# Pooled queries transposed by DMA, eight lanes for the MoE tail, and shorter score bursts chosen by backlog, in a fused attention and MoE kernel

## The chip, the cores and the metric

One core of a Trainium2 chip runs the whole program. The metric is the device time of one execution in microseconds (us). The span in a profile is 1.7 to 1.8 us shorter than that time. Runs of one kernel differ by 1 to 2% (39 runs of the kernel before in one job: 403.58 to 410.49 us), and with one core a run counts as slow when it is over 1.5% above the fastest of its kernel; only fast runs are compared. Ratios are the mean time of one kernel's fast runs over the mean of the other kernel's fast runs of the same rounds, so they are not quite the ratios of the medians quoted beside them.

## The reference

```python
# q, k, v: (8, 8, 1152, 64);  x: 4608 tokens x 512;  w1, w2: 512 x 1024;  w_out: 1024 x 512
q_pool = q.reshape(B, H, S // 2, 2, D).mean(axis=3)               # 576 queries a head
scores = scale * np.matmul(q_pool, k.transpose(0, 1, 3, 2))
attn = softmax(scores)                                            # (max, exp, sum)
x = np.matmul(attn, v).transpose(0, 2, 1, 3).reshape(B * 576, 512)
g = np.maximum(x @ w1, x @ w2)
out = g @ w_out
```

## The kernel before

Thirty-two pairs of heads, four pairs to a batch, run through TensorE (PE), the exponential on ScalarE (ACT), and PE again. Pooled queries, keys and values are prepared by GpSimd (POOL). As soon as a batch is through attention, its 576 tokens become MoE work, in blocks of 512 tokens. The kernel writes `max(x w1, x w2) w_out` as `relu(x (w1 - w2)) w_out + x (w2 w_out)`, so the MoE has a first layer ("h" jobs) and an output ("p" jobs).

The kernel uses eight PSUM banks of 512 FP32 columns. Six are three score buffers of two banks; two are "lanes" for everything else. The order in which PE does things is fixed when the program is built, by a greedy scheduler with its own rough clock:

```python
sps = [psum([P, 2, 512], f"sps{g}") for g in range(3)]     # score buffers
fb = [psum([P, 512], f"fb{g}") for g in range(2)]          # lanes

def qtrans(i):                 # pooled queries of pair i, transposed by PE through a lane
    def go(e, m):
        for u in range(QU):    # 9
            last = e.transpose(mb[:, u * HP:(u + 1) * HP], qp[s][:, u, :, :]..., ident[0:HP, 0:HP])
    def evac(m):
        dve(lambda e: e.tensor_copy(qpT[s][:, :], mb[:, 0:SQ]), ...)

def scores(g):                 # one group: 512 score columns for each of two heads, 64 rows each
    for i, t, lo, hi, col in pieces(g):
        for h in range(2):
            e.matmul(sps[r][:, h, col:col + hi - lo], kT[i % 3][rows(h), t, :], qpT[i % 2][rows(h), lo:hi], ...)

while p_end[0] < NTOK:
    # ... fill both lanes from the queues
    ready, stall = burst_now(BURST)               # BURST = 3 groups
    if ready and stall <= 0.1:                    # all their score buffers (nearly) free
        emit_burst(ready)
    elif fresh:                                   # else a piece of lane work that can start now
        emit_unit(...)
    else:
        # ... a smaller burst, if it saves more than 0.25 us of waiting
```

The softmax here doesn't subtract the row's maximum and nothing guards it: scores larger than these inputs give would overflow.

## Time and profile before

| | before |
|---|---|
| time, median of 3 runs | 407.5 us (406.59 to 410.68) |
| span of the profiled run, mean granted clock | 405.7 us, 0.992 |
| PE, ACT, DVE busy | 93%, 78%, 38% of the span |
| last scores end, last matmul ends | 346.8 us, 401.6 us |
| bursts of scores, by the built order | 118 |

The page gives averages over three stages with different limits: the start (to about 60 us, waiting for loads), the stretch in which attention and MoE share PE (to 346.8 us), and the tail of MoE alone. The lines on which this rests stand in the prediction below.

### The profile page before, as it was taken

How to read it: one execution, taken by the hardware profiler on the slowest of the kernel's cores; microseconds unless marked ns; L12 is line 12 of the kernel's file. 1: busy time of each engine (PE TensorE's matmuls, PEld its weight loads, DVE VectorE, ACT ScalarE, POOL GpSimd, SP SyncE). 2: the span in 40 equal slices, each digit the busy share in tenths (PEclk: the TensorE clock that was granted, in tenths of full speed). 3: DMA queues.
4: the chain of work that ended last, by engine and by line, in shares of the span. 5: the costliest groups of instructions: out<-in, count | busy, mean ns of one | idle time of the engine just before them, and what ended most of it. 6: DMA issues, size and time to landing. Idle time of an engine off the chain costs nothing.

```text
span 405.7 us, 11812 instructions
## 1 busy us (share of the span) xinstructions
PE 379.2 (93%) x5253; PEld 220.9 (54%) x5253; DVE 154.7 (38%) x310; ACT 317.3 (78%) x355; POOL 162.7 (40%) x135
## 2 busy tenths in 40 slices
PE   2886899999999998999999999999999999999895
PEld 1464465646554655565555555556555565544552
DVE  2458635342344333423243324422542244253221
ACT  3975889999998798989999999999999999400220
POOL 1458975526543563426545436435645110000000
PEclk9996999999999999999999999999999999999999
DMA  7999999647399979975799869998993520221322
GB/s 271 411 401 395 396 305 276 209 151 228 84 221 278 374 174 215 326 169 161 141 331 272 228 143 279 300 309 197 246 306 60 107 61 2 52 56 29 75 53 52
DMA packets 77091, 84.63 MB, mean 209 GB/s; under 512 B 49648, under 2 KB 50160, under 8 KB 77040
## 3 DMA queue, kind: packets, MB, share of 16 engines
q1 hardware_dynamic: 77040, 83.87, 74.6%
q8 instruction: 41, 0.67, 0.7%
q14 instruction: 10, 0.08, 0.1%
HBM read 62.91 MB, written 9.44 MB: 178 GB/s over the span
## 4 chain that ended last, share of the span: by engine, by line
PE 83%; DVE 7%; ACT 5%; DMA 3%; issue 1%; SPq 1%
PE fb L598 23%; PE fb L366 21%; PE sps L417 18%; PE fb L571 16%; ACT et L424 5%; PE fb L318 2%; PE fb L536 2%; DMA xT<-xnat 1%; DVE stage L582 1%; DVE wd L508 1%; DMA qraw<-in_q_dram 1%; DVE xnat L378 1%; DVE wo L512 1%; DVE stage L612 1%; PE fb L337 1%
## 5 line engine op out<-in xcount | busy, mean ns | idle before, releaser
L424 ACT ACTIVATE et<-sps 128x1024 bf16<-128x1024 f32 (+1 forms) x336 | 308.2, 998 | 32.4 <-PE sps L417 31.7
L292 POOL TENSOR_TENSOR qp<-qraw 64x576 bf16<-64x576 f32 x62 | 88.7, 1431 | 79.9 <-PE fb L318 65.6
L417 PE MATMUL sps<-qpT,kT 64*128 64x64 bf16 (+7 forms) x1152 | 98.5, 294 | 7.0 <-ACT et L424 4.3
L366 PEld LDWEIGHTS fb<-vE,et 128*128 128x128 bf16 x2880 | 93.6, 98 | 14.6 <-issue 7.3
L366 PE MATMUL fb<-vE,et 128*128 128x65 bf16 x2880 | 100.0, 194 | 0.1
L571 PE MATMUL fb<-xT,wd 128*128 128x512 bf16 (+3 forms) x352 | 73.9, 342 | 3.4 <-DMA xT<-xnat 0.9
L598 PE MATMUL fb<-wo,stage 128*128 128x512 bf16 x288 | 75.5, 380 | 0.0
L417 PEld LDWEIGHTS sps<-qpT,kT 64*128 64x128 bf16 x1152 | 43.8, 96 | 53.6 <-issue 22.5
L299 POOL TENSOR_SCALAR vE<-vraw 128x1152 bf16<-128x1152 f32 x32 | 38.1, 1191 | 76.2 <-issue 62.2
L582 DVE TENSOR_SCALAR stage<-fb 128x512 bf16<-128x512 f32 (+3 forms) x76 | 47.6, 628 | 40.9 <-PE fb L571 39.8
L376 DVE RECIPROCAL rc<-fb 128x5 f32<-128x5 f32 x64 | 12.5, 195 | 109.3 <-PE fb L366 109.3
L571 PEld LDWEIGHTS fb<-xT,wd 128*128 128x128 bf16 x352 | 28.5, 97 | 38.2 <-DVE stage L582 10.2
L612 DVE COPY stage<-fb 128x512 f32<-128x512 f32 x32 | 22.1, 690 | 57.9 <-PE fb L598 57.5
L598 PEld LDWEIGHTS fb<-wo,stage 128*128 128x128 bf16 x288 | 25.4, 98 | 28.2 <-issue 3.9
L268 POOL TENSOR_SCALAR kbf<-kraw 128x1152 bf16<-128x1152 f32 x31 | 36.2, 1167 | 7.5 <-DMA kraw<-in_k_dram 7.5
L598 PE MATMUL fb<-w,xT 128*128 128x512 bf16 x144 | 37.6, 380 | 0.8 <-DVE xnat L378 0.4
L378 DVE TENSOR_TENSOR xnat<-fb,rc 128x320 bf16<-128x320 f32 x64 | 31.5, 492 | 2.2
L609 ACT COPY stage<-fb 128x512 f32<-128x512 f32 x4 | 2.3, 586 | 31.6 <-PE fb L598 31.6
L325 DVE COPY qpT<-fb 128x576 bf16<-128x576 bf16 x32 | 14.5, 454 | 20.6 <-PE fb L318 20.6
L598 PEld LDWEIGHTS fb<-w,xT 128*128 128x128 bf16 x144 | 12.8, 97 | 17.1 <-DVE xnat L378 1.6
L318 PEld LDWEIGHTS fb<-ident,qp 64*128 64x128 bf16 x288 | 11.2, 97 | 12.7 <-DVE stage L582 4.2
L318 PE MATMUL fb<-ident,qp 64*128 64x64 bf16 x288 | 14.2, 194 | 3.1 <-DVE kT L344 3.1
(27 smaller groups left out, 68.9 us busy)
## 6 DMA issues: line engine op xcount, KB each, us to landing
qraw<-in_q_dram SPq DMA_DIRECT2D x32, 576.0 KB, 5.7
vraw<-in_v_dram SPq DMA_DIRECT2D x32, 576.0 KB, 7.1
kraw<-in_k_dram SPq DMA_DIRECT2D x31, 576.0 KB, 8.3
out_dram<-stage SPq DMA_DIRECT2D x72, 128.0 KB, 2.4
xT<-in_moe_w_dram SPq DMA_DIRECT2D x4, 512.0 KB, 9.5
stage<-in_moe_w_dram SPq DMA_DIRECT2D x4, 512.0 KB, 14.7
stage<-in_moe_w_out_dram SPq DMA_DIRECT2D x4, 512.0 KB, 14.5
xT<-xnat SPq DMA_TRANSPOSE x30, 2.5
```

The lines of the kernel that those rows point to most:

```text
L268: op("POOL", lambda g: g.tensor_scalar(kbf[s][:, :, :, :].rearrange("p t h d -> p h t d"), kraw[r][:, :, :, :], 1.0, 1.0, ALU.mult, ALU.mu ...
L292: op("DVE" if i == 0 else "POOL", lambda g, half=half, a=a: g.tensor_tensor(qp[s][:, :, half, :], a[:, :, 0, :], a[:, :, 1, :], ALU.add), ...
L299: op("POOL", lambda g: g.tensor_scalar(vE[r][:, :, :, 0:D].rearrange("p t h d -> p h t d"), vraw[r][:, :, :, :], 1.0, 1.0, ALU.mult, ALU.m ...
L318: last = e.transpose(mb[:, u * HP:(u + 1) * HP], qp[s][:, u, :, :].rearrange("p h d -> p (h d)"), ident[0:HP, 0:HP])
L366: last = e.matmul(fb[m][:, sb * 66:sb * 66 + 65], et[:, a:a + P], vE[vs][:, t, half, 0:65], start=(t == 0), stop=(t == NT - 1))
L378: dve(lambda e: e.tensor_tensor(xnat[xs][:, :, c:c + D], a[:, :, 0:D], rc[half][:, :].unsqueeze(2).to_broadcast([P, NCH + 1, D]), ALU.mult ...
L417: last = e.matmul(sps[r][:, h, col:col + hi - lo], kT[i % 3][rows(h), t, :], qpT[i % 2][rows(h), lo:hi], start=True, stop=True)
L424: op("ACT", lambda e: e.activation(et2[:, :, c:c + z - a], sps[r][:, :, a - g * W:z - g * W], EXP, scale=scale), r=[f"s{r}"], w=keys + [f" ...
L571: return e.matmul(fb[m][:, 0:size], wd[:, ct, ft * P:(ft + 1) * P], xT[:, ct, n0:n1], start=(ct == 0), stop=(ct == NC_ - 1))
L582: dve(lambda e: e.tensor_scalar_max(gT[:, ft, g0:g0 + size], fb[m][:, 0:size], 0.0), [f"f{m}"], w, 0.1 + size / 960.0)
L598: return e.matmul(fb[m][:, :], lhs, rhs, start=(j == 0), stop=(j == NC_ + NF - 1))
L612: dve(lambda e: e.tensor_copy(osb[o][:, :], fb[m][:, :]), [f"f{m}"], [f"osb{o}", f"f{m}"], 0.63)
```

## The change

The intent has three parts. From the sixth pair on, a DMA transposes the pooled queries, so PE and DVE need not. Once the last scores are done, the six score banks become lanes as well. And a burst holds three groups only while more than 800 tokens of MoE work are waiting, otherwise two. With the third goes a smaller margin: a smaller burst than this is put in when it saves 0.15 us of waiting instead of 0.25. The runs below change rule and margin together, except e10 to e12, which keep the margin. The rest of the diff is bookkeeping (a third buffer for the transposed queries, jobs that may now finish out of order).

```diff
-        qpT = [sbuf([P, SQ], BF16, f"qpT{s}") for s in range(2)]
+        qpT = [sbuf([P, SQ], BF16, f"qpT{s}") for s in range(3)]
+        fb += [sps[g][:, half, :] for g in range(3) for half in range(2)]
+        def qtrans_dma(i):
+            s, z = i % 2, i % 3
+            op("SP", lambda e: e.dma_start_transpose(
+                qpT[z][:, :].rearrange("p (u x) -> p u x", x=HP),
+                qp[s][:, :, :, :].rearrange("p u h d -> p (u h d)")),
+                r=[f"qp{s}.0", f"qp{s}.1"], w=[f"qpT{z}"], dma=f"d_qT{z}", cost=0.8, mode="t")
...
-        BURST = 3
+        LAG = 800
+        Q_PE = 5
...
+                if i + 2 >= Q_PE:
+                    later(f"qp{i % 2}.1", lambda: (qtrans_dma(i + 2), q_done.add(i + 2)), margin=1.5)
...
+        def more_banks():
+            for g in range(3):
+                for half in range(2):
+                    m = 2 + 2 * g + half
+                    lane[m] = None
+                    plan.writer[f"f{m}"] = plan.writer[f"s{g}"]
+                    plan.readers[f"f{m}"] = set(plan.readers[f"s{g}"])
...
+        def burst_size():
+            done = [b for b in range(B) if all(av_half.get(b * NHP + j) == 2 for j in range(NHP))]
+            return 3 if len(done) * SQ - p_end[0] > LAG else 2
...
+            if nxt == NGR:
+                more_banks()
...
-            for kk in (0, 1):
+            for kk in lane:
-            ready, stall = burst_now(BURST)
+            ready, stall = burst_now(burst_size())
...
-                if ready and stall < wait - 0.25:
+                if ready and stall < wait - 0.15:
```

More of the change, by code (lines that the diff above doesn't have):

```diff
@@ L324, in evac @@
                 mb = fb[m][:, :].bitcast(BF16)
-                dve(lambda e: e.tensor_copy(qpT[s][:, :], mb[:, 0:SQ]),
-                    [f"f{m}"], [f"qpT{s}", f"f{m}"], 0.4)
+                dve(lambda e: e.tensor_copy(qpT[i % 3][:, :], mb[:, 0:SQ]),
+                    [f"f{m}"], [f"qpT{i % 3}", f"f{m}"], 0.4)
             return Job("q", [unit([f"qp{s}.0", f"qp{s}.1", "ident"], 0.3, go, "s")], evac, ("q", i))
+        def qtrans_dma(i):
[4 more added lines that the diff above has]
+                r=[f"qp{s}.0", f"qp{s}.1"], w=[f"qpT{z}"], dma=f"d_qT{z}", cost=0.8, mode="t")
         def ktrans_pe(i, cuts=(0, 5, 9)):
@@ L408, in skeys @@
         def skeys(g):
-            return [key for i, t, *_ in pieces(g) for key in (f"kT{i % 3}.{t}", f"qpT{i % 2}")]
+            return [key for i, t, *_ in pieces(g) for key in (f"kT{i % 3}.{t}", f"qpT{i % 3}")]
         def scores(g):
@@ L418, in pe @@
                             sps[r][:, h, col:col + hi - lo], kT[i % 3][rows(h), t, :],
-                            qpT[i % 2][rows(h), lo:hi], start=True, stop=True)
+                            qpT[i % 3][rows(h), lo:hi], start=True, stop=True)
                 return last
@@ L618, in bass_funnel_attn__then__act_maxout2_kernel @@
         entered = -1
-        lane = [None, None]
+        lane = {0: None, 1: None}
         queue = {kind: [] for kind in "qkxawhp"}
@@ L625, in bass_funnel_attn__then__act_maxout2_kernel @@
         h_end = [0]
+        h_ok = [0]
+        p_got = set()
         p_at = [0]
@@ L637, in bass_funnel_attn__then__act_maxout2_kernel, with later @@
         W_AT = (0, 0, 1)
-        BURST = 3
-        def later(key, fn, tag=None):
-            todo.append((plan.writer[key], fn, tag))
+        LAG = 800
+        Q_PE = 5
+        def later(key, fn, tag=None, margin=0.0):
+            todo.append((plan.writer[key], fn, tag, margin))
         def force(tag):
@@ L673, in enter @@
                 cast_q(i + 2)
+                if i + 2 >= Q_PE:
+                    later(f"qp{i % 2}.1", lambda: (qtrans_dma(i + 2), q_done.add(i + 2)), margin=1.5)
             if i + 1 < NPAIR:
                 cast_v(i + 1)
-                queue["q"].append(qtrans(i + 1))
+                if i + 1 < Q_PE:
+                    queue["q"].append(qtrans(i + 1))
             if i + 4 < NPAIR:
@@ L686, in flush @@
             for entry in list(todo):
-                if plan.ops[entry[0]]["seen"] <= now():
+                if plan.ops[entry[0]]["seen"] + entry[3] <= now():
                     todo.remove(entry)
@@ L791, in emit_unit @@
                 h_left[job.nb] = h_left.get(job.nb, NF) - 1
-                if h_left[job.nb] == 0:
-                    h_end[0] = hblocks[job.nb][1]
+                while h_left.get(h_ok[0]) == 0:
+                    h_end[0] = hblocks[h_ok[0]][1]
+                    h_ok[0] += 1
             elif job.kind == "p":
-                p_end[0] = job.nb
+                p_got.add(job.nb)
+                while p_end[0] + P in p_got:
+                    p_end[0] += P
             if job.done:
@@ L835, in bass_funnel_attn__then__act_maxout2_kernel @@
             cand = []
-            for kk in (0, 1):
+            for kk in lane:
                 job = lane[kk]
@@ L850, in bass_funnel_attn__then__act_maxout2_kernel @@
                     wait = min(wait, stall)
-                size = BURST
+                size = burst_size()
                 while size > 1 and (not ready or stall > 0.05):
```

## The prediction

> **What bounds the kernel now.** I read the page's busy shares and slices first, then the table of windows, the waits, the chain in order of time, and last the DMA views.
>
> ```profile
> PE 379.2 (93%) x5253; PEld 220.9 (54%) x5253; DVE 154.7 (38%) x310; ACT 317.3 (78%) x355; POOL 162.7 (40%) x135
> PE   2886899999999998999999999999999999999895
> ACT  3975889999998798989999999999999999400220
> DMA  7999999647399979975799869998993520221322
> ```
>
> PE is at nine tenths or more from slice 6 almost to the end. ACT, which computes the exponentials, is close behind and stops at slice 34; then only MoE work is left. The windows (width, busy time and count of PE, PEld, DVE, ACT and POOL, clock, DMA share, GB/s) say how full PE is:
>
> ```profile
> 80.00:120.00 40.00, 39.77 (x593) 22.97 (x589) 14.27 (x30) 37.70 (x42) 18.65 (x16) 1.00 0.59 172
> 240.00:280.00 40.00, 40.00 (x600) 23.56 (x599) 14.82 (x31) 36.87 (x41) 19.16 (x16) 1.00 1.10 287
> 370.00:380.00 10.00, 9.06 (x64) 4.85 (x62) 1.99 (x5) 2.18 (x6) 0.00 (x0) 1.00 0.35 79
> ```
>
> From 80 us on PE is idle less than 0.3 us in most windows of 40 us, while ACT has 2 to 3 us to spare in each. So the attention stage is bound by PE work, not by ACT, though by a small margin. Whatever is not done by the end of attention is done afterwards at PE's own pace, so the end is a sum of PE time: only PE work taken away, or PE gaps closed, shortens it. ACT's waits for scores are real but sit off the path:
>
> ```profile
> ACT et L424 <- PE sps L417: 31.7, 77, 3.3
> DVE qpT L325 <- PE fb L318: 20.6, 20, 3.4
> ```
>
> The tail is different. The chain after 376 us alternates between matmuls and evacuations:
>
> ```profile
> 376.51 0.41 PE fb L571 x4
> 376.92 0.02 issue
> 376.94 0.30 DVE stage L582
> 377.24 0.05 issue
> 377.29 0.41 PE fb L571 x4
> 377.70 0.02 issue
> 377.72 0.30 DVE stage L582
> ```
>
> With two lanes (two PSUM banks) PE waits for a bank to be emptied before it can start the next short job. The last matmul ends near 401.6 us and the rest of the span, 4.1 us, is the last copy and store.
>
> [...] The score matmuls use 64 rows and the rest 128, so each burst of scores is a mode change in and out. The trace agrees: in the chain a burst of one group takes 0.33 to 0.36 us, of two 0.54, of three 0.76, so 0.215 us per group and 0.11 fixed, and the matmuls that follow a burst are slower by about as much again. [...] a key transpose moves 128 x 1152 x 2 bytes = 295 KB, half of a 576 KB load, yet in the quiet window 85 to 97 us it lands in 3.2 us against 5.3 for a load, and the median over all is 5.5:
>
> ```profile
> xT<-xnat SPq DMA_TRANSPOSE x30, 2.5
> kT<-kbf SPq DMA_TRANSPOSE x27, 5.5
> ```
>
> **Part one, pooled queries transposed by DMA.** Of 32 query jobs on PE, 5 stay and 27 go, each nine transposes and one DVE copy.
>
> ```profile
> L318 PE MATMUL fb<-ident,qp 64*128 64x64 bf16 x288 | 14.2, 194 | 3.1 <-DVE kT L344 3.1
> L325 DVE COPY qpT<-fb 128x576 bf16<-128x576 bf16 x32 | 14.5, 454 | 20.6 <-PE fb L318 20.6
> ```
>
> The row's 14.2 us counts overlapping matmuls; I take the chain instead. Between 44 and 347 us it holds 222 of these transposes in 8.47 us, that is 0.343 us per job of nine. They mostly stand next to a burst of scores, in the same 64-row mode, so no mode change goes with them. 27 x 0.343 = **9.3 us of PE, on the path**. The copies, 27 x 0.454 = 12.3 us, leave DVE, which is 38% busy: no gain of their own, only fewer late evacuations. Added are 27 DMA transposes of 64 x 1152 x 2 = 147 KB on SP's queue, each about 1.3 us of issuing (the shortest key transposes and the transposes of x take 1.2 to 1.4 us to issue), and half a key transpose of data. The order of the built kernel shows them two head pairs ahead of use. A pair takes about 10.6 us, so more than 10 us remain from the end of the POOL addition to the first score matmul, against a landing time of 3 to 8 us.
>
> **Part two, burst size.** The built order has 147 bursts against 118: 92 of two groups and 36 of three, where before 87 were of three. Six of the 29 extra bursts lie before the first transposes of x (64.8 us), where PE is not the bound; 23 lie after. What one costs: the stretch from 64.8 to 346.8 us is 282.0 us. By the built order it holds 274 groups x 0.215 = 58.9; 2430 attention-value matmuls x 0.0303 (45 in 1.36 us) = 73.6; 519 matmuls' worth of 512 columns x 0.2157 = 112.0; 26 query jobs x 0.343 = 8.9; 20 transposes of x = 1.2. The sum is 254.6. PE idles for some 3 us there. The remaining 24.4 us over 99 bursts is 0.25 us per burst, which fits the 0.11 + 0.1 seen directly. So 23 x 0.25 = **+5.8 us**. Against it, smaller bursts wait less for three free score buffers; of PE's 3 us idle in the stretch and its 2.4 us between 40 and 80 us I give back 1.5 us.
>
> **Part three, eight lanes at the end.** After the last scores the six score banks become lanes. The tail from 346.8 to 401.6 us is 54.8 us. Its work by the same rates: 140 output matmuls and 31,232 columns of the first MoE layer (61 x 512) x 0.2157 = 43.4; 90 attention-value matmuls 2.7; transposes 1.1: together 47.2. So 7.6 us are gaps, and the chain's own sum agrees: from 352 us its DVE, ACT and issue pieces other than the last copy come to 10 us, part of it hidden under matmul latency. In the new order fourteen output matmuls and six of the first layer stand between the last attention values and the transposes, and first-layer jobs alternate over banks, so about 1 us of gaps should be left: **-6.5 us**. (Four output matmuls, 0.9 us, move from the tail into the stretch before: no net effect.) Evacuation cannot become the bound: eight copies of 256 columns shared by DVE (0.43 each) and ACT take 1.7 us, their matmuls 3.4.
>
> **Sum.** 405.7 - 9.3 + 5.8 - 1.5 - 6.5 = 394.2 us of span; time runs 1.7 us above span (407.4 against 405.7 in the profiled run). 407.5 - 11.5 = **396.0 us**, 2.8% faster.
>
> **Rivals.** *DMA or SP becomes the bound.* For: the DMA share is above 1 in the window 240 to 280 us, key transposes take up to 5 us to issue in such places, and SP is one queue in order, so a late query transpose delays the next loads. As an estimate, the page's DMA share of 74.6% is 303 us; 72 MB of plain transfers at the first windows' 370 to 400 GB/s are about 190 of it, leaving 110 for 11.5 MB of transposes, so 4.0 MB more could add 38 us, nearly filling the attention stage. Against: that share counts queued time, the loads are three pairs ahead, quiet windows have shares of 0.3 to 0.6, and no score matmul waits for a key transpose in the list of waits. If true: 3 to 10 us of PE stalls, 399 to 406 us. *Only the bursts count.* If a mode change costs more than 0.25 us, or smaller bursts let PE catch up with ACT and wait for it, parts one and two cancel and only the tail is left: about 401 us. *ACT was the hidden bound.* If feeding ACT more evenly moves attention forward and the early, badly filled first 60 us improve too (15.3 us of PE idle before 60 us), 3 to 4 us more come off: 392 us. ACT's 2 to 3 us of slack per 40 us speak against a larger gain.
>
> **Range and chances.** The tail gain is the surest part, the burst cost the least sure (0.15 to 0.35 us gives 3.5 to 8 us), DMA trouble is the one-sided risk. So 391.5 to 402 us. The 2% line is 399.35 us, 3.35 above the prediction: faster 0.77, within 2% 0.21, slower 0.02.
>
> **What would show each step.** Right: the query transposes and their copies fall to 5 jobs; the span up to the last score burst shortens by 4 to 5 us to about 342; the last matmul comes about 48 us after it; PE stays above 39.5 us in each window of 40. The query transposes land within 8 us and no score matmul waits for them. Wrong: PE idle before scores with a DMA of queries or keys as releaser (the DMA rival); PE waiting for ACT in the middle windows (the burst rival); more than 51 us from the last score burst to the last matmul (the lanes). A stretch of attention longer than before would make the whole prediction wrong.

## The result, and the profile after

The changed kernel took 393.17 us (median of 4 runs, 392.38 to 395.84) against 407.11 us for the kernel before: a ratio of 0.9651, 95% interval 0.9579 to 0.9723. A later job with more rounds gave 0.9625 (0.9582 to 0.9669), 391.43 us.

The page of the changed kernel, to be set beside the slices of before:

```profile
PE 366.4 (93%) x4949; PEld 214.9 (55%) x5010; DVE 142.2 (36%) x283; ACT 316.7 (80%) x355; POOL 163.3 (41%) x135
PE   2786999999999999999999999999799999999995
PEclk9766999999999999999999999999899999999999
```

PE is as full as before with 243 transposes fewer; this trace lacks 61 matmul records (4949 of 5010), so its busy time is a little low. The 8 near the end of before is gone, and there is one new dent, the 7 for 276 to 286 us, with a lower clock in the same slice (8 tenths). The same three windows as in the prediction say it in numbers:

```profile
80.00:120.00 40.00, 39.15 (x573) 22.18 (x578) 11.91 (x26) 39.04 (x43) 19.25 (x16) 1.00 0.78 193
240.00:280.00 40.00, 37.59 (x565) 21.89 (x571) 12.26 (x26) 37.53 (x41) 21.66 (x18) 1.00 1.17 282
370.00:380.00 10.00, 10.00 (x47) 4.53 (x47) 1.07 (x2) 1.17 (x2) 0.00 (x0) 1.00 0.37 79
```

ACT is fuller than before (39.04 against 37.70 us in the first), the tail has no idle PE left, and the second window has 2.4 us of it that were not there before. The chain near the end of the changed kernel (start, duration, what):

```profile
365.73 0.44 PE sps L579 x4
366.17 0.87 PE fb L579 x8
367.04 2.18 PE sps L579 x20
369.22 0.05 issue
369.28 5.13 PE fb L606 x23
```

Where the chain of before alternated between a matmul and an evacuation, PE now goes from one bank to the next. Five pieces run 8.7 us without a wait over 0.05 us.

The waits and the DMA view of the changed kernel:

```profile
ACT et L432 <- PE sps L425: 28.8, 43, 3.3
qpT<-qp SPq DMA_TRANSPOSE x27, 6.2
kT<-kbf SPq DMA_TRANSPOSE x27, 6.4
```

From issue to landing a query load (576 KB) takes 5.4 us at the median. The query transposes (147 KB) land in 6.2 us at the median (2.7 to 7.7), and in the list of waits of the changed kernel no score matmul waits for one. The last scores end at 343.2 us (before 346.8), and the last matmul comes 46.7 us later (before 54.8): 3.6 us were gained up to there and 8.1 in the tail.

So the time and the places looked as predicted. Whether each part of the change did what its step said is another question, and two traces cannot answer it.

### The profile page after: what moved, and what is told of

The parts are those of the page before. It is cut to its first block, busy times and chain, and to the rows that moved or that the text cites. A ratio compares the mean times of both kernels' runs of the same rounds, so it can differ in the third digit from the quotient of the medians.

```text
span 394.1 us, 11238 instructions
## 1 busy us (share of the span) xinstructions
PE 366.4 (93%) x4949; PEld 214.9 (55%) x5010; DVE 142.2 (36%) x283; ACT 316.7 (80%) x355; POOL 163.3 (41%) x135
## 4 chain that ended last, share of the span: by engine, by line
PE 87%; ACT 5%; DVE 4%; issue 2%; DMA 1%; SPq 0%
PE fb L374 23%; PE sps L425 20%; PE fb L606 18%; PE fb L579 14%; PE sps L606 5%; ACT et L432 5%; PE sps L579 2%; PE fb L544 1%; DMA qraw<-in_q_dram 1%; DVE xnat L386 1%; PE fb L345 1%; PE fb L528 1%; DVE wd L516 1%; DVE xT L534 1%; DVE xT L513 0%
## 5 line engine op out<-in xcount | busy, mean ns | idle before, releaser
L425 PE MATMUL sps<-qpT,kT 64*128 64x512 bf16 (+7 forms) x1152 | 100.9, 293 | 6.2 <-ACT et L432 4.0
L374 PE MATMUL fb<-vE,et 128*128 128x65 bf16 x2880 | 105.0, 195 | 0.9 <-DVE xnat L386 0.7
L579 PE MATMUL fb<-xT,wd 128*128 128x512 bf16 (+3 forms) x267 | 61.7, 360 | 2.6 <-issue 1.8
L606 PE MATMUL fb<-wo,stage 128*128 128x512 bf16 x200 | 53.6, 380 | 2.7 <-issue 2.1
L590 DVE TENSOR_SCALAR stage<-fb 128x512 bf16<-128x512 f32 (+2 forms) x65 | 42.8, 658 | 34.4 <-PE fb L579 33.6
L579 PEld LDWEIGHTS fb<-xT,wd 128*128 128x128 bf16 x284 | 23.8, 98 | 30.1 <-issue 9.4
L606 PEld LDWEIGHTS fb<-wo,stage 128*128 128x128 bf16 x224 | 19.0, 98 | 23.6 <-issue 6.7
L606 PE MATMUL fb<-w,xT 128*128 128x512 bf16 x100 | 27.7, 380 | 0.7 <-issue 0.3
L586 ACT ACTIVATE stage<-fb 128x256 bf16<-128x256 f32 (+1 forms) x6 | 2.1, 348 | 16.3 <-PE fb L579 16.2
L606 PE MATMUL sps<-wo,stage 128*128 128x512 bf16 x62 | 15.0, 379 | 0.1
L606 PEld LDWEIGHTS sps<-wo,stage 128*128 128x128 bf16 x64 | 6.1, 98 | 7.1
```

Of the source, the lines that this page charges most:

```text
L374: last = e.matmul(fb[m][:, sb * 66:sb * 66 + 65], et[:, a:a + P], vE[vs][:, t, half, 0:65], start=(t == 0), stop=(t == NT - 1))
L425: last = e.matmul(sps[r][:, h, col:col + hi - lo], kT[i % 3][rows(h), t, :], qpT[i % 3][rows(h), lo:hi], start=True, stop=True)
L579: return e.matmul(fb[m][:, 0:size], wd[:, ct, ft * P:(ft + 1) * P], xT[:, ct, n0:n1], start=(ct == 0), stop=(ct == NC_ - 1))
L590: dve(lambda e: e.tensor_scalar_max(gT[:, ft, g0:g0 + size], fb[m][:, 0:size], 0.0), [f"f{m}"], w, 0.1 + size / 960.0)
L606: return e.matmul(fb[m][:, :], lhs, rhs, start=(j == 0), stop=(j == NC_ + NF - 1))
```

## The experiments

All results were correct except where said. Each experiment's edit is against the changed kernel. Two numbers are used throughout. **The store** is how much MoE work, in us of PE, is still startable when the last attention value matmul of a batch has been put in order. It is worked out from the built order: the MoE matmuls of earlier batches not yet done, at 0.2157 us per 512 columns as in the prediction, less those whose block of 512 tokens is not complete. (A recount from the kernels for this text came within 0.2 us of every value.) **Clock loss** is the sum of (1 - granted clock) x 4 us over the windows of 4 us from 44 us to the last scores.

| kernel | bursts | ratio | PE's wait for ACT, 44 to 350 us | clock loss, us | last scores end, us | from there to last matmul, us |
|---|---|---|---|---|---|---|
| before | 118 | 1 | 2.2 | 0 | 346.8 | 54.8 |
| e1 lanes | 118 | 0.9851 | 2.2 | 0 | 344.9 | 47.5 |
| e2 query DMA | 112 | 1.0129 | 10.6 | 3.4 | 345.4 | 54.8 |
| e3 burst rule | 146 | 0.9974 | none listed | 0 | 335.2 | 63.4 |
| e4 lanes + query DMA | 112 | 0.9902 | 10.6 | 6.8 | 352.5 | 47.6 |
| e7 as e2, small copies | 112 | 1.0032 | 10.4 | 5.1 | 350.5 | 54.7 |
| e8 lanes + burst rule | 146 | 0.9741 | none listed | 0 | 337.2 | 55.6 |
| changed (again, e9) | 147 | 0.9625 | 1.4 | 1.7 | 341.0 | 46.7 |
| e10 two for four batches | 140 | 0.9677 | 3.4 | 1.7 | 338.3 | 47.6 |
| e11 always two | 164 | 0.9681 | 1.3 | 0 | 330.9 | 56.5 |
| e12 small store | 122 | 0.9791 | 6.7 | 3.4 | 344.4 | 47.5 |

The last four columns are from the one profiled run of each; that of e4 was a slow one, and those of e1, e2 and e10 were the fastest of their kernels, so these columns don't add up to the ratios.

### e1: the lanes alone

With the lanes gone too, the same edit gives back the instruction order of the kernel before.

```diff
-        Q_PE = 5
+        Q_PE = 99
-            return 3 if len(done) * SQ - p_end[0] > LAG else 2
+            return 3
-                if ready and stall < wait - 0.15:
+                if ready and stall < wait - 0.25:
```

> The kernel before with the eight lanes at the end alone; queries on PE, bursts as before (118). PE-sum theory: the stretch up to the last scores is unchanged (ends near 346.8 us), the tail from there to the last matmul falls from 54.8 to about 48.3 us: 401 us, 6.5 us less. Rival (evacuation binds in the tail): 52 us or more of tail, 404 to 406 us.

Measured: 400.96 us (4 runs), ratio 0.9851 (0.9797 to 0.9905), 6.1 us at 407. The tail was 47.5 us. The prediction's step for the lanes holds.

### e2: the query DMA alone

```diff
-            return 3 if len(done) * SQ - p_end[0] > LAG else 2
+            return 3
-                if ready and stall < wait - 0.15:
+                if ready and stall < wait - 0.25:
-            if nxt == NGR:
-                more_banks()
```

> The kernel before with the query transposes by DMA alone; two lanes, bursts of three. The built order has 112 bursts instead of 118. PE-sum theory: 27 x 0.343 = 9.3 us of transposes and 6 x 0.25 = 1.5 us of mode changes leave PE: about 397 us, the tail unchanged at 55 us. DMA rival: stalls at transposes or loads give back 3 us or more: 400 us or above, with a DMA named ahead of idle PE.

Measured: 410.68 us (4 runs, 3 fast), ratio 1.0129 (1.0061 to 1.0197): no faster, and probably slower, though PE has 9 us less to do. How much slower is less sure than the ratio looks: the mean of the three fast runs is 409.1 us, that of all fast runs of the kernel before in the job 406.6, which is 0.6% or 2.5 us, where the ratio says 5 us. The profiled run is the fastest (406.05 us, mean clock 0.986); the others took 410.1 to 414.0 us at mean clocks of 0.966 to 0.982, so they seem to lose more of what the trace shows. My first thought was the DMA rival, but the idle PE does not wait for a DMA. The timeline of PE near the end of the second batch (start, duration, operation, idle before):

```profile
101.35 0.61 PE L425 MATMUL sps<-qpT,kT 64*128 64x448 bf16 x6
102.46 0.39 PE L425 MATMUL sps<-qpT,kT 64*128 64x512 bf16 x2 [0.50 <-ACT et L432]
103.37 0.39 PE L425 MATMUL sps<-qpT,kT 64*128 64x64 bf16 x4 [0.53 <-ACT et L432]
104.29 0.39 PE L425 MATMUL sps<-qpT,kT 64*128 64x128 bf16 x4 [0.52 <-ACT et L432]
105.21 0.39 PE L425 MATMUL sps<-qpT,kT 64*128 64x192 bf16 x4 [0.53 <-ACT et L432]
106.12 0.39 PE L425 MATMUL sps<-qpT,kT 64*128 64x256 bf16 x4 [0.52 <-ACT et L432]
106.45 3.89 PE L374 MATMUL fb<-vE,et 128*128 128x65 bf16 x72
```

PE has nothing left but scores. It hands ACT one group, waits half a microsecond for a buffer, hands over the next. Then comes a line to look at twice: 72 attention value matmuls take 3.89 us, where the same 72 take 2.35 us in the timeline of before. The windows of the same trace show a lowered clock there (it is the third number from the end):

```profile
100.00:104.00 4.00, 2.74 (x57) 1.71 (x55) 0.69 (x2) 4.00 (x5) 2.43 (x3) 1.00 0.67 169
104.00:108.00 4.00, 2.66 (x41) 1.90 (x42) 0.00 (x0) 4.00 (x6) 2.60 (x2) 0.81 0.53 101
108.00:112.00 4.00, 3.97 (x80) 3.35 (x76) 0.88 (x3) 2.12 (x3) 0.10 (x1) 0.76 0.60 154
```

PE was a third idle for 8 us (2.74 and 2.66 of 4 us busy), the clock was 0.81 in the second window and 0.76 in the third, PE fell behind, and in the last window ACT, which had been full, was only 2.12 of 4 us busy. So in this stretch three losses follow one another: 2.6 us of idle PE, a slow stretch of PE, and time in which ACT starves in turn. That the idle time lowered the clock is my reading of this order; no run tests it. The clock losses in the table are 0, 1.7, 3.4, 5.1 and 6.8 us, multiples of 1.7 as far as the rounding goes; no run shows why.

The store fits the place: by the built order e2 has 0.0 and 0.5 us of startable MoE work at the second and third batch end, before 3.5 and 2.6. With 9 us less work PE caught up with its own supply. A batch's tokens become MoE work only at its end, and until then there is nothing to fill in. Where the clock falls varies: e2, e4 and e7 have the same order up to the tail, but their traces show a lowered clock, in brackets its lowest in a window of 4 us, at 104 (0.76) and 284 us (0.58) in e2, at 108 (0.79), 160 (0.69), 204 (0.73) and 288 (0.67) in e4, and at 156 (0.67), 200 (0.62) and 288 (0.62) in e7. Nor does every idle stretch have one: in e7 PE was 2.85 and 2.55 of 4 us busy in the windows from 104 and 108 us, and the clock was 1.00 in both and in the next.

### e3: the burst rule alone

```diff
-        Q_PE = 5
+        Q_PE = 99
-            if nxt == NGR:
-                more_banks()
```

> The kernel before with the burst rule alone (two or three groups, and the smaller margin); queries on PE, two lanes. The built order has 146 bursts instead of 118, 28 more. PE-sum theory: 22 more in the PE-bound stretch x 0.25 = 5.5 us slower, less up to 2 us of waits: 410 to 413 us. Rival (feeding ACT evenly is what the change gains by): at or below 405 us.

Measured: 405.06 us (20 runs), ratio 0.9974 (0.9949 to 1.0): no slower, where the prediction's step says about 4 us slower; the expectation's 410 to 413 us is ruled out, and its rival's mark of 405 us is met to within 0.1. Attention ended 11.6 us earlier and left 8.6 us more tail: two groups need two free buffers instead of three, so scores come sooner and MoE work is put off. The store at the batch ends 2 to 7 rose to 6.1, 10.4, 11.3, 13.0, 13.0 and 13.9 us.

### e4: the changed kernel without the burst rule

```diff
-            return 3 if len(done) * SQ - p_end[0] > LAG else 2
+            return 3
-                if ready and stall < wait - 0.15:
+                if ready and stall < wait - 0.25:
```

> The changed kernel with bursts of three as before: query DMA and eight lanes stay. 112 bursts instead of 147. PE-sum theory: the sum of the two gains alone, 407 - 10.8 - 6.5 = about 390 us, so 3 us or more faster than the changed kernel (393.2). Rival (the burst rule pays for itself, by less waiting): 394 us or more, slower than the changed kernel.

Measured: 404.62 us (median of 20 runs, of which 11 count as fast), ratio of the fast ones 0.9902 (0.9867 to 0.9937). The rival was right by a wide margin: without the burst rule 10 to 11 us of the gain are gone (0.9902 against 0.9651 and 0.9625 is 2.5 to 2.8% of 407). The runs spread from 398.77 us at a mean clock of 0.986 to 408.45 at 0.961. The order is that of e2 up to the tail, with the same empty store.

### e5 and e6: what does a change of tiling mode cost?

```diff
             # cut: the lines that give back the kernel before, as in e1 and e3
             def pe(e):
+                i, t, lo, hi, col = next(iter(pieces(g)))
+                e.matmul(sps[r][:, 0, col:col + 16], kT[i % 3][:, t, :],          # e6: [rows(0), t, :]
+                         qpT[i % 3][:, lo:lo + 16], start=True, stop=True)        # e6: [rows(0), ...]
                 for i, t, lo, hi, col in pieces(g):
```

Both are the kernel before in its own order; the needless outputs are overwritten.

> The kernel before with one needless matmul of 16 columns over all 128 rows ahead of every group of scores (324 in all, their outputs overwritten by the scores that follow). Inside the bursts they make 206 extra changes of mode there and back (324 groups less 118 bursts). If a change there and back costs 0.25 us as the prediction has it: 206 x 0.25 = 51 us more than the control with 64 rows. If it costs 0.06 us, as the third run suggests: about 12 us more.

> The control: the same 324 needless matmuls over 64 rows, in the mode of the scores, so no extra change of mode. Only their own time, at most 0.06 us each by the shortest spacing in the chain (0.03 us): 10 to 20 us more than the kernel before, under both theories.

Measured: e5 450.24 us, ratio 1.101 (1.0951 to 1.107); e6 412.9 us, 1.0139 (1.0094 to 1.0184). The control was expected at 10 to 20 us more and came out 4 to 6 us slower, so the needless matmuls themselves cost about 0.02 us each. The difference of the medians is 37.3 us, over 206 changes from 64 rows to 128 and back 0.18 us each; by the ratios it is 0.17. A recount of the built order finds 17 changes more, at bursts that follow a query job (64 rows too); over 223 it is 0.16 to 0.17. So a change costs less than the 0.25 us of the prediction and much more than the 0.06 that e3 had made me think of. The remaining 7 us of the 24.4 that the prediction shared out among the bursts belong to something else. The 28 bursts added in e3 therefore cost about 5 us, and e3 must have gained that much and a little more. Where is not broken down: PE's listed waits for ACT, 2.2 us before and none here, are only a part.

### e7: is it the DMA traffic?

```diff
-            op("SP", lambda e: e.dma_start_transpose(
-                qpT[z][:, :].rearrange("p (u x) -> p u x", x=HP),
-                qp[s][:, :, :, :].rearrange("p u h d -> p (u h d)")),
+            op("SP", lambda e: e.dma_start(
+                qpT[z][0:HP, 0:D], qp[s][:, 0, 0, :]),
```

> The second run (queries by DMA, two lanes, bursts of three; 410.7 us) in the same order, but each of the 27 transposes is replaced by a small plain copy of 64 x 64 elements: results wrong on purpose. If DMA traffic of the transposes is what took the gain: about 397 us. If PE starves because its store of MoE work is used up at the batch boundaries (by the built order 2.2 and 4.8 us left at the second and third, before 5.6 and 6.9): it stays within 3 us of 410.7, with PE still waiting over 8 us for ACT.

(The edit shown comes on top of that of e2. The expectation counts all MoE work left; startable of it are 0.0 and 0.5 us.) The result is wrong on purpose. Measured: 411.39 us (11 runs, 7 fast), ratio 1.0032 (0.9985 to 1.0079). With nearly all of the transposes' traffic gone, the kernel was still no faster than the kernel before, and PE's waits stayed (this list covers 44 to 350 us: total, times, longest):

```profile
PE sps L424 <- ACT et L431: 10.4, 21, 0.7
```

The e2 kernel over the whole span, and the kernel before:

```profile
PE sps L425 <- ACT et L432: 12.2, 26, 0.7
```

```profile
PE sps L417 <- ACT et L424: 4.3, 11, 0.7
```

So the traffic of the transposes is not what took the 9 us. Its ratio lies 1% above e7's, but the intervals (1.0061 to 1.0197, and 0.9985 to 1.0079) overlap and the means of the fast runs are alike (409.1 and 409.3 us), so what the traffic itself costs stays open.

e7 does not rule out another effect, the order of SP's queue. The next MoE work needs the five DMA transposes of a batch's x (its tokens after attention). In the traces of before, e1, e3 and e8 SP begins them within 0.6 us after DVE has written the last part of x, mostly within 0.03. In e2 SP first issues a query transpose and, but for the last time, a key load, and begins 1.3 to 2.8 us late at five of six batch ends (the third to the seventh). In e7 it is still 0.6 to 1.7 us late there. So the query DMA also brings new MoE work later, just where PE runs short. No run changes this order alone, so its share of the loss is not known.

### e8: the changed kernel without the query DMA

```diff
-        Q_PE = 5
+        Q_PE = 99
```

> The changed kernel with the queries back on PE: burst rule and lanes stay. By adding the parts alone: 406.7 - 5.9 (lanes) - 1.5 (burst rule) = 399 us. The changed kernel's 393.2 then says that the query DMA is worth about 6 us beside the burst rule, though it costs 4 without. If the parts do not interact, it should instead be near 389.

Measured: 397.44 us (4 runs), ratio 0.9741 (0.9696 to 0.9786). The query DMA is worth 0.9741 against 0.9651 or 0.9625, that is 0.9 to 1.2% or 4 to 5 us, when the burst rule is there, and costs 2 to 5 us when it is not (e2). The tail here is 55.6 us for 55.3 us of work by the rates of the prediction: eight lanes leave next to no gap.

### e9 to e12: is it the store, or the burst size as such?

e9 is the changed kernel again. The others change one line. e10's, `len(done) > 3`, keeps bursts of two until four batches are through, not three as its name and expectation say; its 140 bursts and its stores are those of the edit as it ran.

```diff
-            return 3 if len(done) * SQ - p_end[0] > LAG else 2
+            return 3 if len(done) > 3 else 2           # e10
+            return 2                                   # e11
-        LAG = 800
+        LAG = 400                                      # e12
```

> The changed kernel once more, beside the three that follow: near 393 us, 0.965 of the kernel before.

> The changed kernel with another rule: bursts of two until three batches are through, then of three. 140 bursts against 147, and by the built order 6.1, 10.6 and 16.9 us of MoE work in store at the second to fourth batch end (changed kernel 6.1, 10.8, 13.4). Store theory: no starving, 7 x 0.18 = 1.3 us less of mode changes: 391 to 393 us. Rival (the number of groups in a burst matters all along, for ACT's sake): slower than the changed kernel by 2 us or more, since its last five batches run with bursts of three.

> The changed kernel with bursts of two throughout: 164 bursts, 17 more, store up to 26.9 us. Store theory: 17 x 0.18 = 3 us more of mode changes, no starving: 393 to 397 us. Rival (ACT's feeding all along): 391 us or less.

> The changed kernel with half the backlog limit (400 tokens instead of 800): 122 bursts, 25 fewer, but only 3.5 and 8.2 us in store at the second and third batch end. Mode changes alone: 25 x 0.18 = 4.5 us faster, 389 us. Store theory: PE starves at the second batch end and the clock falls, 395 to 402 us, with PE waiting for ACT near 105 us.

Startable store at the batch ends, us, and where the clock fell below 0.99 after 44 us (in brackets the clock of each window of 4 us):

| kernel | batch end 2 | 3 | 4 | 5 | 6 | 7 | low clock at |
|---|---|---|---|---|---|---|---|
| before | 3.5 | 2.6 | 3.1 | 5.9 | 3.8 | 5.9 | nowhere |
| e2 | 0.0 | 0.5 | 3.1 | 5.7 | 3.1 | 5.7 | 104 to 112 (0.81, 0.76), 284 to 288 (0.58) |
| e8 | 6.1 | 10.4 | 11.3 | 13.0 | 13.0 | 13.9 | nowhere |
| changed | 3.9 | 6.5 | 7.0 | 6.8 | 4.0 | 3.8 | 280 to 288 (0.72, 0.85) |
| e10 | 3.9 | 6.3 | 10.4 | 6.3 | 3.3 | 6.1 | 276 to 284 (0.67, 0.90) |
| e11 | 3.9 | 6.3 | 10.4 | 10.4 | 13.0 | 13.9 | nowhere |
| e12 | 1.3 | 3.9 | 3.1 | 4.2 | 3.1 | 6.2 | 196 to 204 (0.73, 0.84), 280 to 288 (0.90, 0.67) |

Measured: e9 391.43 us, 0.9625 (0.9582 to 0.9669); e10 394.0 us, 0.9677 (0.9636 to 0.9718); e11 393.64 us, 0.9681 (0.9644 to 0.9718); e12 397.83 us, 0.9791 (0.9737 to 0.9845). Six fast runs each.

e12 is the plainest: 25 bursts fewer than the changed kernel should save 4.5 us, but it is 6 to 7 us slower, with PE waiting 6.7 us for ACT and two dips of the clock, both where the store is 3.1 us. The first of them:

```profile
196.00:200.00 4.00, 2.50 (x15) 0.79 (x16) 0.00 (x0) 3.97 (x6) 3.27 (x3) 0.73 0.63 134
200.00:204.00 4.00, 4.00 (x64) 2.52 (x63) 1.38 (x2) 2.35 (x4) 0.00 (x0) 0.84 0.99 243
```

The time is as the store theory said, the place only in part: the dip was expected at the second batch end, near 105 us, where the store is least (1.3 us). There PE did wait 2.3 us for ACT (90 to 120 us), but the clock held at 1.00. e11 lies in the range for the store theory; its 17 extra bursts cost what its fuller store gains. e10 agrees with neither theory clearly: it was expected at 391 to 393 and came out at 394; that is 2.6 us above the median of e9, which is the mark of its rival, but the intervals of the two overlap. None of the variants beats the changed kernel.

The store is not a sharp threshold. The kernel before got by on 2.6 us without a dip, perhaps because its PE had 9 us more to do and ran less far ahead of ACT. Within the kernels with query DMA, each dip after 44 us falls near a batch end with at most 4.0 us in store, though not every such end has a dip. In the changed kernel SP's order fits the difference: the transposes of x begin 3.0 us late (3.2 in e9) at the sixth batch end, which has the dip, 1.1 late at the seventh and at most 0.2 at the earlier ones, though the store is about 4 us at the second, the sixth and the seventh. It is not the whole rule either: at the second batch end of e10 they begin 2.6 us late with 3.9 us in store, and there is no dip (clock 1.00 from 96 to 116 us).

## Why the prediction was right, and where its reasons were not

**The total and the places.** The total was met partly by luck, as the steps show. 396.0 was forecast, with 391.5 to 402.0 as the range; 393.2 and 391.4 were measured. The last scores were forecast at about 342 us and came at 343.2 and 341.0; the last matmul 48 us after, and it came 46.7 us after. Two of the signs named for it failed in one place each: one window of 40 us has less than 39.5 us of busy PE (below), and in e9 the slowest query transpose took 8.7 us to land instead of at most 8.

**Lanes.** Forecast -6.5 us, measured -6.1 (e1) with the mechanism shown in the chain. In the changed kernel the tail shrank by 8.1 us, of which 0.9 are the four output matmuls moved out of it. This step is right.

**Query DMA.** "27 x 0.343 = 9.3 us of PE, on the path" is right about PE and wrong about the path. Alone it gained nothing and probably cost 2 to 5 us (e2), and beside the other parts it brought 4 to 5 us (e8 against the changed kernel). The step that failed is the sentence before all the sums: "only PE work taken away, or PE gaps closed, shortens it". That holds while PE always has something to do. In e2, with PE work taken away, PE ran out of MoE work at the batch ends, waited for ACT (10.6 us, 2.2 before), and its granted clock fell there (to 0.76 and 0.58, 3.4 us of clock loss).

**Burst size.** Forecast as a net loss, +5.8 less 1.5 us. The price of a mode change was too high (0.18 us measured, 0.25 forecast; 23 x 0.18 = 4.1 us), and the gain far too low: alone the rule is neutral (e3), beside the other two it is worth 10 to 11 us (e4). The rival in the prediction that came nearest, feeding ACT more evenly, put 3 to 4 us on it and looked for them in the first 60 us. PE's idle time before 80 us did fall, from 16.2 us to 13.3 in e9, so this rival may hold for a part. What e4, e11 and e12 support for the rest is that the rule works by putting MoE work off, so that PE has a store at each batch end. The total was met because an overrated part and an underrated part nearly cancel: the parts do not add, and the prediction added them.

**DMA rival.** The traffic of the query transposes is not the main cause of e2's loss (e7); the delay in SP's queue may be a part of it. And the changed kernel has one place where a transfer shows. This is its second trace (e9), which has all 5010 matmul records, near the end of the sixth batch:

```profile
275.67 0.39 PE L425 MATMUL sps<-qpT,kT 64*128 64x192 bf16 x4 [0.65 <-ACT et L432]
276.58 0.39 PE L425 MATMUL sps<-qpT,kT 64*128 64x256 bf16 x4 [0.52 <-ACT et L432]
278.64 3.19 PE L579 MATMUL fb<-xT,wd 128*128 128x512 bf16 x8 [1.66 <-issue]
```

```profile
276.00:280.00 4.00, 1.82 (x11) 0.72 (x10) 0.00 (x0) 3.44 (x5) 2.75 (x2) 0.88 0.94 187
280.00:284.00 4.00, 4.00 (x55) 2.53 (x54) 1.38 (x2) 0.92 (x1) 0.00 (x0) 0.69 0.61 179
```

PE waits with the store used up until the sixth batch's x arrives. Its last product was ready at 265.8 us; SP first issued two loads, a query transpose (1.24 us) and another load, and began the five transposes of x at 269.0; they took 8.3 us to issue (8.2 in the kernel before):

```profile
267.03 1.24 SPq L332 DMA_TRANSPOSE qpT<-qp  x1
268.98 8.29 SPq L471 DMA_TRANSPOSE xT<-xnat  x5
```

Idle PE and low clock from 272 to 284 us come to 4.5 us. Apart from this place PE is over 39.7 us busy in each window of 40 us from 40 to 320 us, as forecast. That the query transpose's 1.24 us lengthen this wait is argued from the order, not tested.

**Still open.** What the DMA traffic itself costs; what the late transposes of x cost (a run with SP's order changed would tell); what the lanes are worth with both other parts present (not run); why e10 did not gain from its fewer bursts.

## What to carry to other kernels

Before crediting work taken off a full engine, ask what that engine does when its filler runs out: here the same 9 us of removed PE work cost 2 to 5 us with bursts of three and gained 4 to 5 with the burst rule, which keeps more MoE work in store for the batch ends. Where one engine fills the gaps of another, let the feeding of the other go first while the store is low, even at the price of more mode changes (0.16 to 0.18 us each here, e5 against e6). And read the granted clock beside each idle spot: in e2 a PE that was a third idle for 8 us went on at a clock of 0.76 in the window that followed.
